# A written-out schedule that counts the port of VectorE and GpSimd, with some work moved between engines

## The chip, the cores and the metric

The kernel runs on one core of a Trainium2 chip. Five engines take part: TensorE (PE, with its weight loads as PEld) multiplies matrices, VectorE (DVE), ScalarE (ACT) and GpSimd (POOL) work element by element, SyncE (SP) issues transfers. Each runs its own instructions in the order in which they were written down and waits for others by semaphores. The metric is device microseconds of one execution; lower is better.

## The reference

Block-sparse attention, whose output is the input of a two-layer network with a Mish-like gate. In short:

```python
scores = (1 / np.sqrt(64)) * q @ k.T                # 4 batches, 8 heads, 768 positions, 64 wide
# block 32; own and neighbouring blocks, first and last row and column of blocks,
# and 3 sampled blocks for each block of queries are kept, the others masked
attn = softmax(np.where(mask, scores, -1e9))
x = (attn @ v).transpose(0, 2, 1, 3).reshape(3072, 512)
h = x @ w_in                                        # 512 x 2048
g = h * np.tanh(np.log1p(np.exp(h)))
out = (g @ w_out).astype(np.float32)                # 2048 x 512
```

q, k and v come as float32, both weights as float64 (two 32-bit words a number).

## The kernel before, in words

Every product is made of float16 matmuls: each factor is scaled by a power of two and split into a high part and a low part (the rest after the high part), and three of the four products are summed. Splitting a number takes a scaling, a cast to float16 and a subtraction, and these steps are shared out among ScalarE, VectorE and GpSimd.

**Attention** is cut into 52 jobs, 13 for each of four batches. A job handles two blocks of 32 queries (or one, "dense", for the first and last block of a batch, over all 768 keys): scores s (L627), maxima mx (L674, dense L669), the negative scaled maximum nb (L685 on ScalarE or L687 on VectorE), exponentials pt (L697), transposes t (L633), high and low parts ph and pl of the transposed weights (L720; L724 on VectorE, or for the first APL jobs a correcting matmul L728 and a copy L733), the product with v into obank (L759), the division xs (L781), a transpose tx, and the parts xh and xl of the network's input (L806, L809). Sampled keys are gathered by GpSimd, for early jobs also by ScalarE, into kg (L564, L561); sampled values by DMAs into vg.

**The weights.** The first (wi) has eight pieces, the second (wo) sixteen. VectorE turns each from float64 into float32 (three steps, L843, L846 and L849). TensorE sums the squares (gram, L327), `root` makes two powers of two from the sum (L358, L361, L235; the same for q, k and v), then each piece is scaled (wt), its high part cast and its low part subtracted. For wi, `split_i` does that by L901 on GpSimd (ScalarE or VectorE where they are freer), L906 or L908, and L910 on GpSimd; pieces with a number below LPE get the subtraction from TensorE instead (wd, L918 and L919) and a copy out of PSUM by ScalarE (L921). For wo it is `parts_o`, with the subtraction L962 on GpSimd. tp_wo is the sum of squares of all of wo: nothing of wo can be scaled, and no second layer begun, before it.

**The network** runs over twelve stages of 256 rows (three a batch): h in 16 halves (L1001, twelve matmuls each), hs, the gate us in five steps on ScalarE, VectorE and GpSimd (L1024 to L1034), g's high and low part (L1042, L1045), and y in 16 halves (L1060). A half of y is of the stage before, and stands between halves of h.

**Order.** All instructions are collected as tasks with a duration, an engine (or several to choose from, "also"), what they read and write, and buffers from rings of fixed size. `Plan.emit` then runs a small model of the engines in the kernel's build and writes out the instructions in the order in which its tasks start; among tasks that can start at the same time the smaller key is first. `pace` spreads the jobs' scores over the network's halves, and delays the first 14 by a table START. Where TensorE would sit idle in the first 200 us of the plan, `fill` writes filler matmuls (L1247) whose result nobody reads. The model's times decide nothing on the chip but the order and the engine.

In the model before, a task marked `port` on VectorE is 1.3 times as long while GpSimd is busy, and a GpSimd task 1.15 times while VectorE is:

```python
if port and free.get("POOL", 0.0) > start:
    t.dur *= 1.3
elif t.eng == "POOL" and free.get("DVE", 0.0) > start:
    t.dur *= 1.15
```

## Time and profile before

| | us |
|---|---|
| timed runs (3): median, lowest, highest | 804.93, 799.87, 806.57 |
| profiled execution: its own time | 797.3 |
| its span, first to last instruction | 795.5 |
| TensorE busy (matmul) | 738.7 (93%) |
| VectorE, ScalarE, GpSimd busy | 522.6, 544.1, 337.2 |

The span is about 2 us shorter than the execution's time. Times in rows are microseconds from the span's start unless marked ns; "x16" counts instructions; L12 is line 12 of the kernel. A row's part after "|" or in brackets is idle time just before these instructions and the instruction that ended most of it. An instruction that holds its engine and is kept from running counts as busy in the profile: it shows as a longer duration, not as idle time.

### The profile page before, as it was taken

To read this page: it belongs to the slowest core of one execution; us is meant where nothing else is said; L and a number is where in the kernel's file an instruction comes from. 1 tells how busy PE (TensorE), PEld (TensorE's weight loads), DVE (VectorE), ACT (ScalarE), POOL (GpSimd) and SP (SyncE) were. 2 spreads that over 40 slices of the span, in tenths; PEclk is the share of its full clock that TensorE was granted. 3 is DMA by queue.
4 is the path that set the end of the run, shared out by engine and by line. 5 is a ranking of instruction groups with operands and counts; after the bars stand their busy time and mean duration, and the time that the engine had idled before them with its cause. 6 is when DMAs were issued, how large, how long until landed. Compare 5 with 4: busy or idle time off the path is not lost.

```text
span 795.5 us, 30849 instructions
## 1 busy us (share of the span) xinstructions
PE 738.7 (93%) x12896; PEld 524.1 (66%) x12896; DVE 522.6 (66%) x904; ACT 544.1 (68%) x859; POOL 337.2 (42%) x392
## 2 busy tenths in 40 slices
PE   6677787699999999999999999998999999999997
PEld 4455576566677776766677676666777667666653
DVE  6689989988976656568576756874776644323230
ACT  3456666788876876887777777877876675555550
POOL 2057775476833534435334543354443421303031
PEclk9899899999999999999999999999999999999999
DMA  8787765405444355235334553263344303000000
GB/s 281 262 256 235 208 205 158 158 2 150 132 119 123 97 162 160 91 83 176 90 81 119 154 160 107 79 180 88 90 117 133 108 25 106 15 14 14 14 14 26
DMA packets 57743, 95.33 MB, mean 120 GB/s; under 512 B 8323, under 2 KB 20612, under 8 KB 57604
## 3 DMA queue, kind: packets, MB, share of 16 engines
q1 hardware_dynamic: 50880, 76.32, 32.7%
q10 hardware_dynamic: 6724, 17.05, 6.6%
q8 instruction: 101, 1.65, 0.9%
q14 instruction: 38, 0.31, 0.1%
HBM read 80.38 MB, written 12.95 MB: 117 GB/s over the span
## 4 chain that ended last, share of the span: by engine, by line
PE 74%; DVE 11%; DMA 7%; issue 3%; ACT 3%; SPq 2%; POOL 1%; ACTq 0%; DVEq 0%; POOLq 0%
PE y L1060 28%; PE h L1001 26%; PE obank L759 6%; PE t L633 6%; PE s L627 4%; DMA raw_q<-in_q_dram 2%; PE obank L1247 1%; PE tx L633 1%; DVE wo L846 1%; DVE wo L849 1%; DVE wt L957 1%; SPq L588 1%; DVE wo L843 1%; DMA vg<-vd 1%; DMA wr<-in_moe_w_in_dram 1%
## 5 line engine op out<-in xcount | busy, mean ns | idle before, releaser
L1001 PE MATMUL h<-xh,wi 128*128 128x256 f16 x1536 | 282.2, 273 | 0.0
L1060 PE MATMUL y<-wo,g 128*128 128x512 f16 x1152 | 277.2, 379 | 0.8 <-POOL wo L962 0.7
L1001 PEld LDWEIGHTS <-wi 128*128 128x128 f16 x2304 | 223.3, 98 | 47.8 <-issue 2.6
L1001 PE MATMUL h<-xl,wi 128*128 128x256 f16 x768 | 209.3, 273 | 0.6 <-issue 0.6
L1045 POOL TENSOR_TENSOR g<-hs,g 128x1024 f16<-128x1024 f32 x48 | 109.9, 2290 | 222.5 <-DVE g L1042 186.7
L1060 PEld LDWEIGHTS <-g 128*128 128x128 f16 x1152 | 110.6, 98 | 101.8 <-issue 3.4
L564 POOL COPY kg<-kt 128x256 f16 x249 | 117.6, 510 | 121.4 <-PE s L627 113.7
L1010 ACT ACTIVATE hs<-h,gsc 128x512 f32<-128x512 f32 x96 | 65.6, 684 | 80.9 <-PE h L1001 73.4
L697 ACT ACTIVATE pt<-s,nb,ns 128x256 f32<-128x256 f32 (+1 forms) x208 | 107.1, 583 | 6.7 <-DVE wi L908 3.2
L720 ACT ACTIVATE ph<-t 128x512 f16<-128x512 f32 x112 | 66.7, 596 | 49.8 <-PE t L633 45.5
L724 DVE SCALAR_TENSOR_TENSOR pl<-t,ph 128x512 f16<-128x512 f32 x97 | 66.2, 684 | 43.7 <-ACT ph L720 43.6
L1034 DVE SCALAR_TENSOR_TENSOR hs<-us,hs 128x1024 f32<-128x1024 f32 x48 | 63.7, 1328 | 28.4 <-ACT us L1033 27.9
L633 PE MATMUL t<-ident,pt 128*128 128x128 f32 x448 | 70.5, 281 | 4.7 <-ACT pl L733 2.4
L1028 DVE TENSOR_SCALAR us<-us 128x1024 f32<-128x1024 f32 x48 | 39.3, 819 | 44.9 <-ACT us L1024 44.9
L633 PEld LDWEIGHTS t<-ident,pt 128*128 128x128 f32 x448 | 51.6, 142 | 18.2 <-ACT pl L733 3.9
L759 PEld LDWEIGHTS <-ph 128*32 128x32 f16 x3584 | 48.2, 95 | 18.9 <-issue 13.5
L674 DVE TENSOR_REDUCE mx<-s 128x4 f32<-128x1024 f32 x44 | 53.3, 1212 | 6.0 <-PE s L627 6.0
L1030 POOL TENSOR_TENSOR us<-us 128x1024 f32<-128x1024 f32 x18 | 36.3, 2018 | 47.3 <-DVE us L1028 41.7
L1024 ACT ACTIVATE us<-hs,hsc 128x1024 f32<-128x1024 f32 x48 | 55.2, 1149 | 1.5 <-DVE hs L1034 0.5
L759 PE MATMUL obank<-vg,ph 128*32 128x65 f16 (+1 forms) x3200 | 50.6, 197 | 2.7 <-issue 2.7
L1032 ACT ACTIVATE us<-us 128x1024 f32<-128x1024 f32 x48 | 50.7, 1055 | 3.0 <-POOL us L1030 2.1
L627 PEld LDWEIGHTS <-q 64*32 64x32 f16 x3024 | 33.7, 92 | 28.6 <-issue 24.9
(201 smaller groups left out, 970.9 us busy)
## 6 DMA issues: line engine op xcount, KB each, us to landing
vg<-vd SPq DMA_DIRECT2D x320, 65.0 KB, 2.4
vg<-vd SPq DMA_DIRECT2D x80, 195.0 KB, 3.0
wr<-in_moe_w_in_dram ACTq DMA_DIRECT2D x8, 1024.0 KB, 7.0
wor<-in_moe_w_out_dram ACTq DMA_DIRECT2D x16, 512.0 KB, 6.5
vd<-v SPq DMA_DIRECT2D x12, 520.0 KB, 3.9
vg<-vd SPq DMA_DIRECT2D x12, 520.0 KB, 4.3
raw_k<-in_k_dram SPq DMA_DIRECT2D x12, 512.0 KB, 5.2
raw_q<-in_q_dram SPq DMA_DIRECT2D x12, 512.0 KB, 4.4
```

Of the source, the lines that this page charges most:

```text
L564: nc.gpsimd.tensor_copy(out=dst, in_=tl["kt", b][:, :, ds(j, BS)])
L627: nc.tensor.matmul(s[g][i * BS:(i + 1) * BS, c0 + cs.start:c0 + cs.stop], q[gs, c * NPR + i, qs], src[gs, a * NPR + i, ks], start=first an ...
L633: nc.tensor.matmul(out, src, ident, start=start, stop=stop, is_transpose=True)
L697: ex = lambda o, x, g, w: nc.scalar.activation(out=o, in_=x, func=AF.Exp, bias=nb[:, g, w:w + 1], scale=tl["ns", b, sus[w]["qb"] // TB][:, ...
L720: nc.scalar.activation(out=new(sb, "ph", ("ph", i, j), [P, 2, 2, P], F16), in_=tl["t", i, j], func=AF.Copy, scale=PSC)
L724: nc.vector.scalar_tensor_tensor(out=new(sb, "pl", ("pl", i, j), [P, 2, 2, P], F16), in0=tl["t", i, j], scalar=PSC, in1=tl["ph", i, j], op ...
L759: nc.tensor.matmul(o[cs, w, g, 0:v1 - v0], p[:, k, g, cs], vt[:, k, 2 * c + g, v0:v1], start=j == 0 and g == 0 and k == 0 and n == 0, stop ...
L1001: nc.tensor.matmul(h[:, f2].rearrange("p (s q) -> p s q", q=BS), wi[:, fp, w, cc, fs], x[:, :, cc], start=f2 == 0 and k == 0, stop=f2 == 1 ...
L1010: nc.scalar.activation(out=tl[kq][:, 2 * (fp % 2):2 * (fp % 2) + 2], in_=tl[kh], func=AF.Copy, scale=gsc[:, fp:fp + 1])
L1034: add("DVE", 1.32, lambda: nc.vector.scalar_tensor_tensor(out=hs(), in0=us(), scalar=-0.5, in1=hs(), op0=ALU.add, op1=ALU.mult), r=[ku], w ...
L1045: add("POOL", 2.3, lambda: nc.gpsimd.tensor_tensor(out=g()[:, 1], in0=hs(), in1=g()[:, 0], op=ALU.subtract), r=[kq, ("gh", b, t, k)], w=[kg])
L1060: nc.tensor.matmul(tl[ky], tl["g", b, t, k][:, g, f, q], wo[:, fc, w], start=fc == 0 and n == 0, stop=fc == NFC - 1 and n == 2)
```

## The change

- The model knows a port: a task of VectorE marked `port` and every task of GpSimd start only when the other engine's held task has ended (or at the end of a small part of it, for a task made of several short ones: `port=0.4`). The factors 1.3 and 1.15 go. Some durations and the model of DMA queues are corrected, and more alternatives of VectorE are marked.
- nb is always made by ScalarE.
- `root` writes the masked exponent back into PSUM and takes both powers from there, so that each of its three steps reads PSUM; before, two read SBUF.
- Scaling wi is done by ScalarE or VectorE, no more by GpSimd; LPE is 10, so that all eight pieces of wi get their low parts by TensorE's subtraction and ScalarE's copy.
- The low parts of wo may be made by VectorE.
- Numbers: WHOLE 14 to 13 (first job whose window of keys is copied by VectorE), APL 7 to 4, START, the keys AT0, ATV and ATP, and for the second batch the jobs at which k, v and q are prepared, PREP (8, 2, 7) to (7, 1, 6): counted from a batch's end, so each one job later.

```diff
-        t = Task({eng: (dur, fn, port), **{e: (d, f, False) for e, d, f in also}}, key, lat, new, kind, len(self.tasks))
+        t = Task({eng: (dur, fn, port or (eng == "POOL" and dur)), **{e: (d, f, o) for e, d, f, o in also}}, key, lat,
+                 new, kind, len(self.tasks))
...
+    def port(held, eng, start, port):
+
+        other = {"DVE": "POOL", "POOL": "DVE"}.get(eng)
+        if port and other in held:
+            at, dur, grain = held[other]
+            if at <= start < at + dur:
+                return at + dur if grain is True else min(at + dur, start + grain)
+        return start
...
-                    start = max(at, f)
+                    start = self.port(held, eng, max(at, f), t.ways[eng][2])
...
+            if port:
+                held[t.eng] = start, t.dur, port
...
-            if port and free.get("POOL", 0.0) > start:
-                t.dur *= 1.3
-            elif t.eng == "POOL" and free.get("DVE", 0.0) > start:
-                t.dur *= 1.15
...
-        nc.vector.tensor_scalar(
-            out=inv.bitcast(I32), in0=tl[key].bitcast(I32), scalar1=1, scalar2=EXPO,
-            op0=ALU.logical_shift_right, op1=ALU.bitwise_and)
-        nc.vector.tensor_single_scalar(
-            inv.bitcast(I32), inv.bitcast(I32), float((64 + sq) << 23), op=ALU.add)
-        pow2_scale(inv, scale)
+        e = tl[key].bitcast(I32)
+        nc.vector.tensor_scalar(out=e, in0=e, scalar1=1, scalar2=EXPO, op0=ALU.logical_shift_right, op1=ALU.bitwise_and)
+        nc.vector.tensor_single_scalar(inv.bitcast(I32), e, float((64 + sq) << 23), op=ALU.add)
+        nc.vector.tensor_scalar(out=scale.bitcast(I32), in0=e, scalar1=-1.0, scalar2=float((267 - 64 - sq) << 23),
+                                op0=ALU.mult, op1=ALU.add)
...
-    WHOLE = 14
+    WHOLE = 13
     SPLIT = 11
-    APL = 7
+    APL = 4
...
-        add("ACT", 0.25 * len(wq), lambda: nb_fn("ACT"), r=[kmx] + [("ns", b, t) for t in qts], w=[("nb", i)],
-            new=[("nb", ("nb", i))], key=-1.5, also=[("DVE", 0.35 * len(wq), lambda: nb_fn("DVE"))])
+        add("ACT", 0.28 * len(wq), nb_fn, r=[kmx] + [("ns", b, t) for t in qts], w=[("nb", i)],
+            new=[("nb", ("nb", i))], key=-1.5)
...
-        add("POOL", 1.4, lambda: t_fn("POOL"), r=[ksc, ("wi", k)], w=[kt], new=[("raw", kt)], key=cls,
-            also=[("ACT", 1.16, lambda: t_fn("ACT")), ("DVE", 0.8, lambda: t_fn("DVE"))])
+        add("ACT", 1.16, lambda: t_fn("ACT"), r=[ksc, ("wi", k)], w=[kt], new=[("raw", kt)], key=cls,
+            also=[("DVE", 0.75, lambda: t_fn("DVE"), True)])
...
-        add("POOL", 1.45, lambda: nc.gpsimd.tensor_tensor(out=wo[:, fc, 1], in0=tl[kt], in1=wo[:, fc, 0],
-                                                          op=ALU.subtract), r=[kt], w=[("wo", fc)], key=cls)
+        sub = lambda eng: eng.tensor_tensor(out=wo[:, fc, 1], in0=tl[kt], in1=wo[:, fc, 0], op=ALU.subtract)
+        add("POOL", 1.2, lambda: sub(nc.gpsimd), r=[kt], w=[("wo", fc)], key=cls,
+            also=[("DVE", 0.7, lambda: sub(nc.vector), True)])
...
-    LPE = 1
-    AT0, ATV, ATW = -15.0, -19.0, 1.0
+    LPE = 10
+    AT0, ATV, ATW = -24.0, -7.0, 1.0
...
-            PREP = (6, 4, 3) if b else (8, 2, 7)
+            PREP = (6, 4, 3) if b else (7, 1, 6)
...
-            LOADO, ATO, ATP = [("dec", 6)], -1.0, -15.0
+            LOADO, ATO, ATP = [("dec", 6)], -1.0, -26.0
...
-    RES, START = 155.0, [0, 66, 57, 72, 72, 57, 99, 72, 15, 12, 9, 24, 6, 18]
+    RES, START = 155.0, [0, 48, 48, 63, 60, 39, 84, 81, 30, 42, 9, 30, 45, 63]
```

More of the change, by code (lines that the diff above doesn't have):

```diff
@@ L145, in emit @@
             if t.kind and t.kind[0] == "dma":
-                dma[t.eng] = max(dma.get(t.eng, 0.0), end) + t.kind[1]
+                other = max([x for e, x in dma.items() if e != t.eng], default=0.0)
+                at = max(dma.get(t.eng, 0.0), end)
+                dma[t.eng] = at + t.kind[1] + min(t.kind[1], 0.5 * max(other - at, 0.0))
                 t.end = max(dma[t.eng], end + t.lat)
@@ L231, in attn_mish_kernel @@
     nc.scalar.preload_act_table_set("natural_log_exp_and_others")
-    def pow2_scale(inv, scale):
-        nc.vector.tensor_scalar(
-            out=scale.bitcast(I32), in0=inv.bitcast(I32),
-            scalar1=-1.0, scalar2=float(267 << 23), op0=ALU.mult, op1=ALU.add)
     offk = const.tile([1, NB * NR], I32, name="offk")
@@ L489, in parts @@
             add("ACT", 1.13, lambda: scaled("ACT"), r=[ks], w=[kr], key=cls,
-                also=[("POOL", 1.15, lambda: scaled("POOL"))])
+                also=[("POOL", 1.15, lambda: scaled("POOL"), 1.15)])
             add("ACT", 1.07, lambda: hi_of("ACT"), r=[kr] + ([("ends",) + key] if what == "v" else []), w=[kh],
@@ L493, in parts @@
                 use=use + ([key] if what != "k" else []), key=cls,
-                also=[("DVE", 0.8, lambda: hi_of("DVE"))])
+                also=[("DVE", 0.75, lambda: hi_of("DVE"), True)])
             add("POOL", 2.15, lo_of, r=[kr, kh], w=[key, ("done",) + key], use=use, key=cls)
@@ L565, in gather_k @@
         add("POOL", 0.53 * NR, lambda: fn("POOL"), r=KT3(b) + ["off"], w=[("kg", n)], use=[("kt", b)], key=-3,
-            also=[("ACT", 0.55 * NR, lambda: fn("ACT"))] if su["early"] else ())
+            port=0.4, also=[("ACT", 0.55 * NR, lambda: fn("ACT"), False)] if su["early"] else ())
         if su["whole"]:
@@ L569, in gather_k @@
                 out=kgs[n][:, :, 0:WK], in_=tl["kt", b][:, :, (qb - 1) * BS:(qb + 2) * BS]),
-                r=KT3(b), w=[("kw", n)], use=[("kt", b)], key=-2)
+                r=KT3(b), w=[("kw", n)], use=[("kt", b)], key=-2, port=True)
     def gather_v(su):
@@ L899, in t_fn @@
                 nc.scalar.activation(out=t, in_=a0_i(k), func=AF.Copy, scale=sc())
[L900 to L901 removed]
             else:
                 nc.vector.tensor_scalar(out=t, in0=a0_i(k), scalar1=sc(), scalar2=None, op0=ALU.mult)
[L904 to L905 removed]
+        add("ACT", 1.16, lambda: t_fn("ACT"), r=[ksc, ("wi", k)], w=[kt], new=[("raw", kt)], key=cls,
+            also=[("DVE", 0.75, lambda: t_fn("DVE"), True)])
         add("ACT", 1.1, lambda: nc.scalar.activation(out=hi, in_=tl[kt], func=AF.Copy), r=[kt],
             w=[("wi", k), ("wih", k)], key=cls,
[L908 removed]
+            also=[("DVE", 0.75, lambda: nc.vector.tensor_copy(out=hi, in_=tl[kt]), True)])
         if k >= LPE:
@@ L931, in load_o @@
         add("ACT", 0.45, lambda: load_w(sb, raw, "raw", w_out.rearrange("(c p) f -> p c f", p=P)[:, fc], a0_o(fc)),
-            r=after, w=[raw, ("wo", fc)], new=[("raw", raw)], key=-5, lat=2.0, kind=("dma", 2.2))
+            r=after, w=[raw, ("wo", fc)], new=[("raw", raw)], key=-5, lat=2.0, kind=("dma", 1.95))
     def piece_o(fc, cls):
@@ L1030, in moe_g @@
         add("POOL", 2.0, lambda: nc.gpsimd.tensor_tensor(out=us(), in0=us(), in1=us(), op=ALU.mult), w=[ku],
-            also=[("ACT", 1.07, lambda: nc.scalar.activation(out=us(), in_=us(), func=AF.Square))])
+            also=[("ACT", 1.07, lambda: nc.scalar.activation(out=us(), in_=us(), func=AF.Square), False)])
         add("ACT", 1.07, lambda: nc.scalar.activation(out=us(), in_=us(), func=AF.Ln, bias=1.0), w=[ku])
@@ L1043, in moe_g @@
         add("DVE", 0.75, lambda: g_fn("DVE"), port=True, r=[kq, "open"], w=[("gh", b, t, k)], new=[("g", kg)],
-            also=[("ACT", 1.07, lambda: g_fn("ACT"))])
+            also=[("ACT", 1.07, lambda: g_fn("ACT"), False)])
         add("POOL", 2.3, lambda: nc.gpsimd.tensor_tensor(out=g()[:, 1], in0=hs(), in1=g()[:, 0], op=ALU.subtract),
@@ L1078, in moe_y @@
             add("DVE", 0.76, lambda: ys_fn("DVE"), r=[ky, ("osc", b)], w=[kys], new=[("ys", kys)], key=-3,
-                also=[("ACT", 0.7, lambda: ys_fn("ACT"))])
+                also=[("ACT", 0.7, lambda: ys_fn("ACT"), False)])
             add("SP", 0.4, out_fn, r=[kys], lat=2.0, kind=("dma", 1.1))
```

29 lines of the change are left out of this document (11 added, 18 removed).

## The prediction

> **What bounds the kernel now.** I read the stretches first. In the windows view the columns are busy time of TensorE (matmul, then weight load), VectorE, ScalarE and GpSimd, with the count of instructions behind each, the granted TensorE clock, the DMA share and GB/s.
>
> ```profile
> core 0: us, PE busy (x) PEld busy (x) DVE busy (x) ACT busy (x) POOL busy (x), PEclk, DMA share, GB/s
> 0.00:50.00 50.00, 32.06 (x602) 25.82 (x603) 34.16 (x84) 22.45 (x39) 9.81 (x26) 0.93 0.82 269
> 50.00:151.00 101.00, 76.31 (x1965) 59.47 (x1962) 94.30 (x145) 65.48 (x120) 65.72 (x58) 0.93 0.68 203
> 151.00:160.25 9.25, 8.30 (x121) 7.40 (x121) 7.89 (x16) 7.39 (x15) 6.38 (x4) 1.00 0.34 117
> 160.25:796.00 635.75, 622.04 (x10216) 431.44 (x10215) 386.27 (x662) 448.74 (x687) 255.26 (x305) 1.00 0.33 95
> ```
>
> There are two regimes. From 160.25 us on TensorE is busy for 622.04 of 635.75 us: only 13.7 us are to be had there, and what VectorE or GpSimd do in it is covered. Before that VectorE is the full engine, 94.30 of 101 us between 50 and 151, while it turns both weight matrices into f32 and serves ten jobs of attention. So the end is the moment at which TensorE becomes full, plus some 636 us of work that stays. These rows of the TensorE timeline date that moment: the scale of the second weight (tp_wo), filler matmuls behind it, and the first matmul of the second layer.
>
> ```profile
> 150.79 0.38 PE L353 MATMUL tp_wo<-am_wo,ones 128*128 128x1 f32 x2
> ...
> 153.21 3.34 PE L1247 MATMUL obank<-neg 128*128 128x240 f16 x31 [0.71 <-DVE xs L781]
> ...
> 160.25 1.46 PE L1060 MATMUL y<-wo,g 128*128 128x512 f16 x6
> ```
>
> Next I read what VectorE's 94.30 us hold, in the groups of 50 to 151 us by form (count | busy us, mean ns).
>
> ```profile
> L849 DVE SCALAR_TENSOR_TENSOR wo<-wor,wo 128x512 int32<-128x512 int32 x16 | 17.1, 1082 | 0.0
> L846 DVE SCALAR_TENSOR_TENSOR wo<-wor,wo 128x512 int32<-128x512 int32 x16 | 16.3, 1028 | 0.0
> L843 DVE TENSOR_SCALAR wo<-wor 128x512 int32<-128x512 int32 x16 | 13.2, 835 | 3.8 <-DMA wor<-in_moe_w_out_dram 3.7
> ...
> L849 DVE SCALAR_TENSOR_TENSOR wi<-wr,wi 128x1024 int32<-128x1024 int32 x4 | 7.0, 1746 | 0.0
> ...
> L361 DVE TENSOR_SCALAR iv_i<-iv_i 128x2 int32<-128x2 int32 x3 | 3.2, 1061 | 0.1
> ...
> L687 DVE TENSOR_SCALAR nb<-mx,ns 128x2 f32<-128x2 f32 x2 | 2.2, 1148 | 0.0
> ```
>
> The same forms, when nothing is in their way, in VectorE's timeline (start us, us):
>
> ```profile
> 49.63 0.18 DVE L361 TENSOR_SCALAR iv_i<-iv_i 128x2 int32<-128x2 int32 x1
> ...
> 61.20 1.23 DVE L849 SCALAR_TENSOR_TENSOR wi<-wr,wi 128x1024 int32<-128x1024 int32 x1
> ...
> 100.23 0.68 DVE L846 SCALAR_TENSOR_TENSOR wo<-wor,wo 128x512 int32<-128x512 int32 x1
> ...
> 105.19 0.22 DVE L687 TENSOR_SCALAR nb<-mx,ns 128x4 f32<-128x4 f32 x1
> ...
> 129.20 0.41 DVE L843 TENSOR_SCALAR wo<-wor 128x512 int32<-128x512 int32 x1
> ```
>
> Group by group, busy less count times the short form: L849 wo 17.1 - 16 x 0.68 = 6.2, L846 wo 16.3 - 10.9 = 5.4, L843 wo 13.2 - 16 x 0.41 = 6.6, L849 wi 7.0 - 4 x 1.23 = 2.1, L361 3.2 - 3 x 0.18 = 2.7, L687 2.2 - 2 x 0.22 = 1.8. That is 24.8 us in which VectorE holds an instruction and does not run it. What it waits for shows where the two timelines are laid side by side:
>
> ```profile
> 70.43 3.08 POOL L910 TENSOR_TENSOR wi<-wt_i,wi 128x1024 f16<-128x1024 f32 x1
> ```
>
> ```profile
> 71.46 2.21 DVE L687 TENSOR_SCALAR nb<-mx,ns 128x2 f32<-128x2 f32 x2
> ```
>
> Two scalings of 128x2 numbers end at 73.67, just behind GpSimd's subtraction, which ends at 73.51. So an instruction of one engine stands still while the other holds what they share. GpSimd's groups between 50 and 151 us:
>
> ```profile
> L564 POOL COPY kg<-kt 128x256 f16 x36 | 20.8, 608 | 10.0 <-PE s L627 7.6 <-POOL kg L564 1.3 <-issue 0.6
> L910 POOL TENSOR_TENSOR wi<-wt_i,wi 128x1024 f16<-128x1024 f32 x7 | 17.6, 2521 | 6.1 <-ACT wi L906 4.1 <-DVE wi L908 2.1
> L901 POOL TENSOR_SCALAR wt_i<-wi,ws 128x1024 f32<-128x1024 f32 x8 | 12.4, 1558 | 2.8 <-DVE wo L849 2.2 <-DVE r L778 0.3 <-DVE ws L235 0.3
> L1030 POOL TENSOR_TENSOR us<-us 128x1024 f32<-128x1024 f32 x3 | 6.0, 1990 | 5.1 <-DVE us L1028 5.1
> L488 POOL TENSOR_TENSOR q<-raw_q,q 128x1024 f16<-128x1024 f32 x2 | 5.1, 2540 | 1.0 <-DVE q L484 1.0
> L1045 POOL TENSOR_TENSOR g<-hs,g 128x1024 f16<-128x1024 f32 x2 | 4.3, 2131 | 7.3 <-DVE wo L849 6.0 <-DVE g L1042 1.2
> ```
>
> **The change, part by part.** *First weight's low parts.* All eight pieces now go the way that one went: GpSimd loses L910 (17.6 us) and L901 (12.4). On GpSimd, in the stretch where pieces 6 and 7 stood, before and then after (wt_i a scaled piece, q a query tile, kg gathered keys; the changed file's line numbers are up to nine higher):
>
> ```order
> L564 COPY kg_111<-kt_237 128x8x32
> L901 TENSOR_SCALAR wt_i_3510<-wi,ws_3303 128x1024
> L901 TENSOR_SCALAR wt_i_3538<-wi,ws_3303 128x1024
> L488 TENSOR_TENSOR q_2_3542<-raw_q_2_2212,q_2_3542 128x1024
> L910 TENSOR_TENSOR wi<-wt_i_3510,wi 128x1024
> ```
>
> ```order
> L571 COPY kg_111<-kt_228 128x8x32
> L480 TENSOR_SCALAR raw_q_2_2252<-raw_q_2_2252,sc_q_2_3543 128x1024
> L495 TENSOR_TENSOR q_2_3643<-raw_q_2_2252,q_2_3643 128x1024
> L540 TENSOR_LOAD offk
> L571 ISA
> ```
>
> The long instructions of the weight are gone; one scaling of a query (ScalarE's before) has come. Up to tp_wo, counted in the two orders, GpSimd also does one L1030 less and 9 copies more. On TensorE the subtractions take places where fillers (neg) stood; the place is behind the transpose of the third job's output (tx), before and after:
>
> ```order
> L728 LDWEIGHTS neg
> L728 MATMUL t_0_2019<-ph_0_2124,neg 128x512
> L633 MATMUL tx_2174<-ident,xs_2015 128x128 x2
> L1247 LDWEIGHTS neg
> L1247 MATMUL obank<-neg 128x240
> ```
>
> ```order
> L640 MATMUL tx_2205<-ident,xs_2082 128x128 x2
> L919 MATMUL wd_0_2209<-wt_i_1858,ident 128x512
> L920 LDWEIGHTS neg
> L920 MATMUL wd_0_2209<-wi,neg 128x512
> L640 MATMUL t_1_2245<-ident,pt_1980 128x128 x4
> ```
>
> So real work replaces fillers, ahead of the next job's transposes (t). Its price, with ScalarE's copies:
>
> ```profile
> 58.38 1.12 PE L918 MATMUL wd<-wt_i,ident 128*128 128x512 f32 x2
> 59.34 0.38 PE L919 MATMUL wd<-wi,neg 128*128 128x512 f16 x1
> ```
>
> ```profile
> L906 ACT ACTIVATE wi<-wt_i 128x1024 f16<-128x1024 f32 x5 | 5.3, 1056 | 0.0
> L685 ACT ACTIVATE nb<-mx,ns 128x4 f32<-128x4 f32 (+1 forms) x9 | 2.5, 289 | 2.1 <-DVE mx L672 2.1
> ...
> L921 ACT ACTIVATE wi<-wd 128x512 f16<-128x512 f32 x2 | 1.3, 630 | 0.0
> ```
>
> A half piece holds TensorE from 58.38 to 59.72, 1.34 us; 14 more make 19 us. Up to 160.25 TensorE is idle for 160.25 - 32.06 - 76.31 - 8.30 = 43.6 us, and the order before holds 186 fillers there at 3.34/31 = 0.11 us, 20 us more. That cover of 64 us hides the 19; without it they would cost 19. ScalarE gets 14 x 0.63 = 8.8 us, 6 scaled pieces at about 1.06 (the nearest row, L906) and 3 more nb at 0.29, and loses 6 pl, 9 gathers and 2 L906: a few us net on an engine busy for 88 of 151.
>
> *Maxima on ScalarE alone, powers of two from PSUM.* VectorE loses nb; behind its mx stands one ScalarE instruction more (0.29) ahead of the exponentials, in a queue with room. On VectorE, behind the third pair of pieces, before and after (tp_w the sum in PSUM, iv_i and ws the two powers, wr and wor raw weights):
>
> ```order
> L687 TENSOR_SCALAR nb_2334<-mx_2208,ns_0_299 128x2
> L687 TENSOR_SCALAR nb_2334<-mx_2208,ns_1_1336 128x2
> L908 CAST wi<-wt_i_2126 128x1024
> L849 SCALAR_TENSOR_TENSOR wi<-wr_1684,wi 128x1024
> L778 TENSOR_SCALAR r_2421<-obank 128x4
> L779 RECIPROCAL r_2421<-r_2421 128x4
> L781 TENSOR_TENSOR xs_2424<-obank,r_2421 128x256
> L358 TENSOR_SCALAR iv_i<-tp_w_2321 128x2
> L361 TENSOR_SCALAR iv_i<-iv_i 128x2
> L235 TENSOR_SCALAR ws_2440<-iv_i 128x2
> ```
>
> ```order
> L781 TENSOR_SCALAR r_2434<-obank 128x4
> L782 RECIPROCAL r_2434<-r_2434 128x4
> L784 TENSOR_TENSOR xs_2437<-obank,r_2434 128x256
> L846 TENSOR_SCALAR wo<-wor_2254,wo 128x512
> L849 SCALAR_TENSOR_TENSOR wo<-wor_2254,wo 128x512
> L367 TENSOR_SCALAR tp_w_2376<-tp_w_2376 128x2
> L368 TENSOR_SCALAR iv_i<-tp_w_2376 128x2
> L369 TENSOR_SCALAR ws_2471<-tp_w_2376 128x2
> L852 SCALAR_TENSOR_TENSOR wo<-wor_2254,wo 128x512
> ```
>
> nb is gone, the three steps of the powers all read PSUM, and the second weight's decode has moved up around them. What reading PSUM costs on 128x2 numbers:
>
> ```profile
> L358 DVE TENSOR_SCALAR iv_i<-tp_w 128x2 int32<-128x2 int32 x3 | 0.4, 147 | 0.0
> ```
>
> 147 ns from PSUM against 0.18 us from SBUF in the L361 row above: no dearer, so I book 0 for the move and count the blocked 2.7 us under the port. [...]
>
> *What VectorE takes on.* Up to tp_wo the order after has, of the forms below, 6 pl more, 7 xl (4 of them half size), one xs, 2 scalings and 2 casts of 1024 columns, and one us (0.68), one hs, one cast of q (0.68) and three nb (0.22) less.
>
> ```profile
> L1034 DVE SCALAR_TENSOR_TENSOR hs<-us,hs 128x1024 f32<-128x1024 f32 x3 | 3.6, 1213 | 0.0
> ...
> L724 DVE SCALAR_TENSOR_TENSOR pl<-t,ph 128x512 f16<-128x512 f32 x6 | 4.1, 677 | 0.0
> L781 DVE TENSOR_TENSOR xs<-obank,r 128x256 f32<-128x256 f32 x8 | 3.4, 424 | 0.3
> ...
> L908 DVE CAST wi<-wt_i 128x1024 f16<-128x1024 f32 x3 | 2.0, 681 | 0.0
> ...
> L809 DVE TENSOR_TENSOR xl<-tx,xh 128x256 f16<-128x256 f32 x1 | 0.4, 408 | 0.0
> ```
>
> 6 x 0.68 + (4 x 0.25 + 3 x 0.41) + 0.7 (0.42 and its two small steps) + 4 x 0.68 = 9.7; less 0.68 + 1.21 + 0.68 + 0.66 = 3.2. Net 6.5 us more.
>
> *What the port gives back.* GpSimd's long instructions (all groups above but the copies) sum to 45.4 us; after, 45.4 - 17.6 - 12.4 - 2.0 + 1.1 = 14.5, a ratio of 0.32. With the copies, 65.72 falls to about 65.72 - 30.0 - 2.0 + 1.1 + 9 x 0.6 = 40, a ratio of 0.61. Waiting left on VectorE: 24.8 x 0.32 = 8 to 24.8 x 0.61 = 15. I take 11, nearer to the long ones, since a copy lasts 0.6 us and cannot hold anybody for 2. Given back: 24.8 - 11 = 14 (10 to 17). That the plan now moves work out of a hold's way is not booked separately; a bad guess of it costs no more than the upper end.
>
> *From tp_wo to the first y.* Before, 9.5 us pass, with two halves of h (twelve matmuls each) and 37 fillers. After, no filler and four halves stand there, since two fewer are done by tp_wo (14 of 18). What a half takes, in the chain that ended last:
>
> ```profile
> 764.32 1.31 PE h L1001 x12
> ```
>
> Without a wait four halves take 5.2 us; with the waits of before, which the halves then fill, it stays 9.5. I take the middle, 7.3: 2.2 less.
>
> *The rest.* Five of sixteen low parts of the second weight go to VectorE, two y-evacuations and squares change engines, preparation of the second batch starts one job later: all behind 160 us, where TensorE waits 13.7 us in all; I book 0, with 3 us either way. The cover there is VectorE's 250 idle us; if the later preparation failed it, TensorE would wait on v of the second batch, which the order after has moved one job back as well.
>
> **Sum.** 6.5 - 14 - 2.2 = -9.7, so TensorE is full at about 150.5 instead of 160.25. VectorE's idle 15.8 of the first 50 us, in which it waits for loads and TensorE, I leave as it is, with 5 us either way for the new order. The profiled execution took 797.3 us (795.5 from first to last instruction): 797.3 - 9.7 = 787.6. The three timed runs lie 2.6 to 9.3 above it, their median 7.6, so I predict 795.
>
> **Rivals.** *The gain turns into another wait (0.32).* L843 already waits 3.7 us for the second weight's transfers, which land in a ring of six tiles that scaled pieces use too; the DMA share is 0.82, then 0.68. A VectorE that is 8 us quicker finds them not there; what stays is 0 to 5 us: 792 to 797 profiled, 800 to 805 as a median. For it speaks that row, against it that 3.7 of 151 us is little.
>
> *Slower: pieces 6 and 7 come late (0.13).* GpSimd finished the last piece early:
>
> ```profile
> 117.48 2.13 POOL L910 TENSOR_TENSOR wi<-wt_i,wi 128x1024 f16<-128x1024 f32 x1
> ```
>
> at 119.6, 31 us ahead of tp_wo. After, they are scaled, cast, subtracted and copied near the end of the front, in queues that run in order: 2 x 1.06 + 1.06 + 4 x 1.34 + 4 x 0.63 = 11 us, plus as much of ScalarE's exponentials standing between, 22 in all; the first layer's products need them, and behind those stands everything on TensorE. If they are 24 us late against need, 797.3 - 9.7 + 24 = 811.6, median 819. It decides from 18 us late (9.7 + 8) on. For it: their place in the order. Against it: VectorE's decode is still running then and is itself the later one.
>
> *The change misses its aim (0.05):* waits stay at 24.8 us because VectorE's decode with two SBUF inputs meets copies instead: 6.5 - 2.2 = 4 us more, 801.6 profiled, 809.
>
> **Chances.** The forecast's case has 0.50, its own range 783 to 801 as a median (10 to 17 given back, 5.2 to 9.5, and the 5 and 3 us left open). About 1% (8 us) is what a measurement of this kernel can tell from no change: faster below 797, slower above 813. Faster: 0.42 of the forecast's 0.50 and 0.05 of the first rival, 0.47. Slower: the second rival's 0.12 and a little of the third, 0.13. Same: 0.40. The range of 782 to 809 leaves out 0.06 below (all waits gone) and 0.13 above.
>
> **What would show it.** Right: L1060 starts near 150.5; L843, L846 and L849 of wo near 0.45, 0.75 and 0.75 us mean; GpSimd busy about 40 us in the stretch before tp_wo; TensorE's idle time after the first y still near 14 us. Wrong: the same means with L843 waiting on wor for 10 us (first rival); h waiting behind wd or L921's copies (second); L849 of wo still above 1 us (third). A TensorE that idles over 20 us after the first y would break the assumption that the rest stays.

## The result, and the profile after

The changed kernel takes 795.75 us (median of seven executions, 792.79 to 796.49), the kernel before, on the same chip, 803.21 (796.62 to 806.57): a ratio of 0.9899, with a 95% interval of 0.9865 to 0.9934. A second series gave 794.33 us and 0.9896 [0.9862, 0.993]. Two single executions of the series below were slow ones (868.18 us with the first matmul of each wd out, 794.91 us with squares and loads later); the medians in the table include them, the ratios do not. So the change is about 1% faster, at the border of what I had called "faster", and the forecast of 795 us is met. The sum behind it is not: I had forecast 787.6 us for the profiled execution, and it took 795.1, only 2.2 less than the one before; a second pair of profiles, below, differs by 6.5.

The first view of after is the page's head and its busy times.

```profile
span 793.4 us, 30780 instructions
PE 745.1 (94%) x12869; PEld 526.1 (66%) x12869; DVE 491.1 (62%) x895; ACT 551.1 (69%) x881; POOL 305.3 (38%) x386
```

VectorE and GpSimd have lost 31.5 and 31.9 us of busy time (522.6 and 337.2 before), TensorE has 6.4 us more. Next the windows of after, cut at tp_wo and at the first matmul of the second layer (columns as in the prediction), and the two rows of TensorE's timeline that give the cuts.

```profile
0.00:50.00 50.00, 32.68 (x605) 26.80 (x606) 37.17 (x88) 22.27 (x34) 10.41 (x27) 0.93 0.89 287
50.00:153.50 103.50, 84.49 (x1998) 61.70 (x1998) 77.43 (x153) 67.10 (x124) 36.03 (x51) 0.93 0.66 198
153.50:159.06 5.56, 5.56 (x54) 5.02 (x53) 4.16 (x10) 5.40 (x11) 3.97 (x2) 1.00 0.09 33
159.06:794.00 634.94, 622.40 (x10218) 432.60 (x10215) 372.38 (x646) 456.29 (x714) 254.89 (x307) 1.00 0.33 95
```

```profile
153.46 0.28 PE L360 MATMUL tp_wo<-am_wo,ones 128*128 128x1 f32 x2
...
159.06 1.46 PE L1062 MATMUL y<-wo,g 128*128 128x512 f16 x6
```

The rest behind the first y is what it was: 622.40 us of TensorE work where it was 622.04. What differs in this pair lies in front. There VectorE's busy time fell from 34.16 + 94.30 = 128.5 to 37.17 + 77.43 = 114.6 us, but tp_wo comes 2.7 us later than before: VectorE's idle time up to tp_wo rose from 22.5 to 38.9 us. Only the way from tp_wo to the first y became shorter, 9.5 to 5.6 us. VectorE's groups of 50 to 153.5 us show both halves of this (count | busy us, mean ns | idle time before, and what ended it):

```profile
L852 DVE SCALAR_TENSOR_TENSOR wo<-wor,wo 128x512 int32<-128x512 int32 x16 | 12.1, 760 | 0.0
L849 DVE SCALAR_TENSOR_TENSOR wo<-wor,wo 128x512 int32<-128x512 int32 x16 | 11.8, 740 | 0.1
L846 DVE TENSOR_SCALAR wo<-wor 128x512 int32<-128x512 int32 x16 | 8.8, 551 | 3.4 <-DMA wor<-in_moe_w_out_dram 3.4
L681 DVE TENSOR_REDUCE mx<-s 128x4 f32<-128x1024 f32 x7 | 8.5, 1220 | 4.4 <-PE s L634 4.4
L727 DVE SCALAR_TENSOR_TENSOR pl<-t,ph 128x512 f16<-128x512 f32 x12 | 8.2, 685 | 13.2 <-ACT ph L723 13.1
L852 DVE SCALAR_TENSOR_TENSOR wi<-wr,wi 128x1024 int32<-128x1024 int32 x4 | 5.4, 1362 | 0.0
...
L368 DVE TENSOR_SCALAR iv_i<-tp_w 128x2 int32<-128x2 int32 x3 | 0.5, 159 | 0.1
L367 DVE TENSOR_SCALAR tp_w<-tp_w 128x2 int32<-128x2 int32 x3 | 0.5, 159 | 0.4 <-PE tp_w L358 0.4
L369 DVE TENSOR_SCALAR ws<-tp_w 128x2 int32<-128x2 int32 x3 | 0.4, 149 | 0.0
```

The waits at the port are nearly gone. By the prediction's own short forms, the decode of wo is over by 12.1 - 10.9 = 1.2, 11.8 - 10.9 = 0.9 and 8.8 - 6.6 = 2.2 us, that of wi (L852) by 0.5, and the scalings of 128x2 numbers by nothing: 4.8 us, where it had been 24.8. But VectorE now stands 13.1 us in front of pl, waiting for a ph of ScalarE; before, that wait did not show. GpSimd's groups of the same stretch:

```profile
L571 POOL COPY kg<-kt 128x256 f16 x44 | 23.5, 543 | 35.5 <-PE s L634 27.5 <-POOL kg L571 5.2 <-issue 1.8
L1032 POOL TENSOR_TENSOR us<-us 128x1024 f32<-128x1024 f32 x2 | 4.5, 2271 | 2.6 <-DVE us L1030 2.6
L1047 POOL TENSOR_TENSOR g<-hs,g 128x1024 f16<-128x1024 f32 x2 | 4.3, 2132 | 9.5 <-ACT g L1042 6.6 <-DVE g L1044 2.9
L495 POOL TENSOR_TENSOR q<-raw_q,q 128x1024 f16<-128x1024 f32 x2 | 4.3, 2131 | 6.3 <-ACT q L489 6.3
```

The 30 us of the first weight are gone, and most of what is left are copies.

Why is ScalarE late? Here are the issue of a load by SyncE (SPq) and the instruction of ScalarE that needs it, first in the timeline of before, then of after. raw_q is the first tile of queries of the second batch, L318 and L325 sum its squares.

```profile
95.14 0.41 SPq L385 DMA_DIRECT2D raw_q<-in_q_dram  x1
...
102.70 1.06 ACT L318 ACTIVATE I-3366_3367<-raw_q 128x1024 f16<-128x1024 f32 x1 [1.34 <-DMA raw_q<-in_q_dram]
```

```profile
102.30 0.41 SPq L392 DMA_DIRECT2D raw_q<-in_q_dram  x1
...
109.73 1.06 ACT L325 ACTIVATE I-3422_3423<-raw_q 128x1024 f16<-128x1024 f32 x1 [6.76 <-DMA raw_q<-in_q_dram]
...
111.40 0.69 DVE L727 SCALAR_TENSOR_TENSOR pl<-t,ph 128x512 f16<-128x512 f32 x1 [4.72 <-ACT ph L723]
```

By the numbers in `load` the plan reckons under 3 us from issue to landing (0.5 to issue, then 1.95 of transfer or 2.0 of latency, whichever ends later), and puts the squares right behind that. On the chip this load takes 7.4 us, and in after it leaves SyncE 7.2 us later than before, behind gathers of vg. ScalarE had ended its other work at 102.97. It is held at the head of its queue by a transfer, while the ph behind it could have run from 105.5 us on, when its transposes were done; and VectorE, which reaches pl in its own order, stands too, for 4.7 of its 13.1 us (another 5.5 lie at 85 us, behind a second stand of ScalarE that comes further down).

The ph is not all that stands behind the squares: so do three of ScalarE's issues of w_out loads, which left at 109.8 and 110.8. The chain of work that ended last goes by these loads (start us, us, what):

```profile
102.30 7.41 DMA raw_q<-in_q_dram
109.82 3.79 DMA wor<-in_moe_w_out_dram
113.63 0.43 DVE wo L846
...
117.58 4.31 PE h L1003 x24
...
128.20 2.73 PE h L1003 x24
```

The last two rows are two halves of h each, so the same work: the first pair took 1.6 us longer, at a granted clock of 0.61; the second ran at 1.00. That ScalarE's stand is what the gain went into was the theory to test.

### The profile page after: what moved, and what is told of

Its sections match the earlier page's. It is cut to its first block, busy times and chain, and to the rows that moved or that the text cites. A ratio compares the mean times of both kernels' runs of the same rounds, so it can differ in the third digit from the quotient of the medians.

```text
span 793.4 us, 30780 instructions
## 1 busy us (share of the span) xinstructions
PE 745.1 (94%) x12869; PEld 526.1 (66%) x12869; DVE 491.1 (62%) x895; ACT 551.1 (69%) x881; POOL 305.3 (38%) x386
## 3 DMA queue, kind: packets, MB, share of 16 engines
q1 hardware_dynamic: 50880, 76.32, 32.6%
## 4 chain that ended last, share of the span: by engine, by line
PE 79%; DVE 7%; DMA 6%; ACT 3%; issue 3%; POOL 2%; SPq 0%; POOLq 0%; ACTq 0%; DVEq 0%
PE y L1062 29%; PE h L1003 28%; PE t L640 6%; PE obank L762 6%; PE s L634 5%; DMA raw_q<-in_q_dram 3%; DMA vg<-vd 2%; PE tx L640 1%; PE obank L1249 1%; DVE hs L1036 1%; POOL wo L963 1%; DMA raw_k<-in_k_dram 1%; DVE wt L958 1%; PE gram_wi L334 1%; DVE wo L852 1%
## 5 line engine op out<-in xcount | busy, mean ns | idle before, releaser
L1047 POOL TENSOR_TENSOR g<-hs,g 128x1024 f16<-128x1024 f32 x48 | 106.2, 2214 | 202.6 <-DVE g L1044 152.6
L571 POOL COPY kg<-kt 128x256 f16 x258 | 114.8, 480 | 170.7 <-PE s L634 156.0
L727 DVE SCALAR_TENSOR_TENSOR pl<-t,ph 128x512 f16<-128x512 f32 x103 | 70.7, 687 | 62.5 <-ACT ph L723 62.2
L1036 DVE SCALAR_TENSOR_TENSOR hs<-us,hs 128x1024 f32<-128x1024 f32 x48 | 66.7, 1391 | 31.9 <-ACT us L1035 31.8
L1032 POOL TENSOR_TENSOR us<-us 128x1024 f32<-128x1024 f32 x19 | 39.2, 2062 | 40.1 <-DVE us L1030 40.1
L1034 ACT ACTIVATE us<-us 128x1024 f32<-128x1024 f32 x48 | 50.7, 1056 | 1.9 <-POOL us L1032 1.3
L1035 ACT ACTIVATE us<-us 128x1024 f32<-128x1024 f32 x48 | 50.7, 1056 | 0.9
```

The lines of the kernel that those rows point to most:

```text
L571: nc.gpsimd.tensor_copy(out=dst, in_=tl["kt", b][:, :, ds(j, BS)])
L727: nc.vector.scalar_tensor_tensor(out=new(sb, "pl", ("pl", i, j), [P, 2, 2, P], F16), in0=tl["t", i, j], scalar=PSC, in1=tl["ph", i, j], op ...
L1036: add("DVE", 1.32, lambda: nc.vector.scalar_tensor_tensor(out=hs(), in0=us(), scalar=-0.5, in1=hs(), op0=ALU.add, op1=ALU.mult), r=[ku], w ...
L1047: add("POOL", 2.3, lambda: nc.gpsimd.tensor_tensor(out=g()[:, 1], in0=hs(), in1=g()[:, 0], op=ALU.subtract), r=[kq, ("gh", b, t, k)], w=[kg])
```

## The experiments

The medians and ratios to the kernel before are of the same series in each row; tp_wo, the first y, the halves of h that TensorE has done by then and its idle time before and behind it are from one profiled execution each.

| kernel | median us | ratio [95% interval] | tp_wo, first y | halves of h | idle before, behind |
|---|---|---|---|---|---|
| before, its first profile | 803.21 | | 150.8, 160.3 | 18 | 43.6, 13.2 |
| before again | 800.54 | 0.9987 [0.9959, 1.0016] | 154.5, 164.0 | 18 | 42.8, 13.1 |
| after | 795.75 | 0.9899 [0.9865, 0.9934] | 153.5, 159.1 | 18 | 36.3, 11.9 |
| after again | 794.33 | 0.9896 [0.9862, 0.993] | 150.8, 156.4 | 18 | 32.1, 11.9 |
| low parts moved, all else as before | 800.78 | 0.9974 [0.9945, 1.0003] | 134.9, 150.3 | 15 | 35.8, 13.0 |
| after, low parts back on GpSimd | 812.29 | 1.0139 [1.01, 1.0177] | 156.2, 167.8 | 16 | 45.5, 16.0 |
| after, port not in the plan | 804.63 | 1.004 [1.0012, 1.0069] | 140.8, 147.2 | 13 | 32.6, 22.8 |
| after, numbers of before | 798.42 | 0.9973 [0.9941, 1.0005] | 142.3, 147.4 | 9 | 33.7, 14.3 |
| after, first matmul of each wd out | 792.74 | 0.9868 [0.979, 0.9946] | 152.8, 158.4 | 18 | 44.2, 10.6 |
| after, squares of another tile | 788.27 | 0.9818 [0.9756, 0.9879] | 148.8, 154.4 | 18 | 30.3, 13.9 |
| after, squares later | 787.05 | 0.9833 [0.9798, 0.9869] | 143.6, 149.2 | 18 | 29.5, 12.0 |
| the same, a second series | 787.41 | 0.9844 [0.9805, 0.9883] | 146.3, 151.9 | 18 | 32.7, 11.2 |
| after, two loads later | 793.59 | 0.9892 [0.9854, 0.993] | 151.6, 157.2 | 18 | 32.4, 12.1 |
| after, squares and loads later | 790.11 | 0.9868 [0.9823, 0.9912] | 143.0, 148.6 | 18 | 28.0, 10.8 |

**The two kernels once more.**

> The kernel before, unchanged. Its timed runs spread from 796.6 to 806.6 us and its profiled execution (797.3) is one of the quick ones. Theory A (the gain lies in the front): ratio 1.000 within 0.004; a second profile shows the first y (L1060) somewhere between 158 and 172 us, and from there to the end 634 to 639 us again, as 635.75 us in the first profile, so that what differs between executions lies ahead of the first y. Theory B (the gain lies behind the first y): the first y again near 160 us, and the stretch behind it longer than 640 us when the execution is slow.

> The changed kernel, unchanged, for a second profile: both theories 0.990 of the kernel before (0.986 to 0.994). Theory A: first y between 156 and 162 us, the rest 634 to 636 us. Theory B: the rest under 634 us.

Profiles of the same kernel differ in front (the first y at 160.3 and 164.0 for before, 159.1 and 156.4 for after) and hardly behind it (635.2 and 634.9; 634.3 and 636.0). So the profile that I started from was a quick execution of before, and the difference of 2.2 us between the two first profiles is less than the 7.5 us between the medians. In the second pair tp_wo comes 3.7 us earlier with the change, where it came 2.7 us later in the first, and the first y 7.6 us earlier instead of 1.2; VectorE's idle time up to tp_wo rises by 10.0 us (26.7 to 36.7) instead of 16.4. The granted clock differs too: from 50 us to tp_wo it was 0.93 in the first profile of before, 0.85 in the second. It is the medians that count below; a single profile tells where, not how much.

**The moved low parts alone**, in the kernel before:

```diff
-        add("POOL", 1.4, lambda: t_fn("POOL"), r=[ksc, ("wi", k)], w=[kt], new=[("raw", kt)], key=cls,
-            also=[("ACT", 1.16, lambda: t_fn("ACT")), ("DVE", 0.8, lambda: t_fn("DVE"))])
+        add("ACT", 1.16, lambda: t_fn("ACT"), r=[ksc, ("wi", k)], w=[kt], new=[("raw", kt)], key=cls,
+            also=[("DVE", 0.8, lambda: t_fn("DVE"))])
...
-    LPE = 1
+    LPE = 10
```

> The kernel before with one part of the change: all eight pieces of the first weight get their low parts from TensorE and ScalarE, and GpSimd no longer scales them; planner, constants, nb and root as before. Theory A: VectorE's decode of the second weight falls to about 0.75, 0.75 and 0.55 us mean (L849, L846, L843; before 1.08, 1.03 and 0.84), and the time to 0.990 to 0.996. Theory C (the planner's model and its numbers make the gain, the first weight is a detail): 0.998 to 1.010, with the plan unfit for the new work on ScalarE.

VectorE's groups of wo in this kernel, 50 to 155 us:

```profile
L846 DVE SCALAR_TENSOR_TENSOR wo<-wor,wo 128x512 int32<-128x512 int32 x16 | 11.4, 719 | 0.0
L849 DVE SCALAR_TENSOR_TENSOR wo<-wor,wo 128x512 int32<-128x512 int32 x16 | 11.4, 720 | 0.0
L843 DVE TENSOR_SCALAR wo<-wor 128x512 int32<-128x512 int32 x16 | 10.1, 631 | 7.2 <-DMA wor<-in_moe_w_out_dram 7.2
```

The waits at the port fall by this move alone, without a plan that knows the port, and tp_wo comes 16 us earlier than before, at 134.9. That is worth nothing measurable: from tp_wo to the first y 15.4 us now pass, and behind the first y there are 649 us instead of 635, since only 15 halves of h, not 18, are done by then. The first y dates the end only between orders that have the same work ahead of it.

**The rest of the change alone**, the low parts back on GpSimd:

```diff
+            elif eng == "POOL":
+                nc.gpsimd.tensor_scalar(out=t, in0=a0_i(k), scalar1=sc(), scalar2=1.0, op0=ALU.mult, op1=ALU.mult)
...
-        add("ACT", 1.16, lambda: t_fn("ACT"), r=[ksc, ("wi", k)], w=[kt], new=[("raw", kt)], key=cls,
-            also=[("DVE", 0.75, lambda: t_fn("DVE"), True)])
+        add("POOL", 1.4, lambda: t_fn("POOL"), r=[ksc, ("wi", k)], w=[kt], new=[("raw", kt)], key=cls,
+            also=[("ACT", 1.16, lambda: t_fn("ACT"), False), ("DVE", 0.75, lambda: t_fn("DVE"), True)])
...
-    LPE = 10
+    LPE = 1
```

> The changed kernel with that part undone: GpSimd scales and subtracts the first weight again (one piece by TensorE), the rest of the change kept, port in the plan included. Theory A: decode means back above 0.9 us, time 0.996 to 1.004 of the kernel before. Theory C: the plan moves the work out of the port's way, decode means 0.75 or less, time 0.988 to 0.994.

Slower by 1.4%, which no theory had: the plan and its numbers do not carry the gain, and without the moved low parts they harm. Yet most of the waits at the port are gone here as well: the decode means are 0.55, 0.71 and 0.87 us, and against the short forms the decode of wo and L852 of wi are about 7 us over, where the same four groups of before were 20.3. So in two kernels, by the move alone and by the plan alone, VectorE got most of these waits back, and neither is measurably faster than before.

**The plan without the port**, and **the numbers of before**:

```diff
-                    start = self.port(held, eng, max(at, f), t.ways[eng][2])
+                    start = max(at, f)
...
+            if t.eng == "DVE" and port and free.get("POOL", 0.0) > start:
+                t.dur *= 1.3
+            elif t.eng == "POOL" and free.get("DVE", 0.0) > start:
+                t.dur *= 1.15
```

> The kernel after, but the planner knows the port as in the kernel before: the start of an instruction is not put off, and its duration is stretched by 1.3 (VectorE) or 1.15 (GpSimd) where the other engine is busy. All operations, the first weight's low parts by TensorE and all constants as in after; only the order moves. Theory P (the plan's knowledge of the port is what makes the moved low parts pay): ratio to before 0.996 to 1.004, VectorE's decode steps in 50 to 150 us back above 0.85 us in the mean, or waits elsewhere that cost as much. Theory Q (knowing the port does nothing once GpSimd has little to do; the numbers and the moved work do it): ratio 0.987 to 0.993, decode steps at 0.55, 0.75 and 0.75 us as in after.

```diff
-    WHOLE = 13
+    WHOLE = 14
...
-    APL = 4
+    APL = 7
...
-    AT0, ATV, ATW = -24.0, -7.0, 1.0
+    AT0, ATV, ATW = -15.0, -19.0, 1.0
...
-            PREP = (6, 4, 3) if b else (7, 1, 6)
+            PREP = (6, 4, 3) if b else (8, 2, 7)
...
-            LOADO, ATO, ATP = [("dec", 6)], -1.0, -26.0
+            LOADO, ATO, ATP = [("dec", 6)], -1.0, -15.0
...
-    RES, START = 155.0, [0, 48, 48, 63, 60, 39, 84, 81, 30, 42, 9, 30, 45, 63]
+    RES, START = 155.0, [0, 66, 57, 72, 72, 57, 99, 72, 15, 12, 9, 24, 6, 18]
```

> The kernel after, but with the numbers of the kernel before for the start of the jobs, the classes of the first weight's pieces and of the second weight's, the job at which the next batch is prepared, and which jobs gather on ScalarE or on VectorE (START, AT0, ATV, ATP, PREP, APL, WHOLE); the first weight's low parts by TensorE and the port in the plan as in after. Theory Q (the numbers had to follow the moved work: what is gained from the port is lost again in the order): ratio to before 0.995 to 1.005, first y at 163 to 168. Theory P (the plan's knowledge of the port makes the order good by itself): ratio 0.987 to 0.993, first y at 156 to 160.

Both lose all or most of the gain. The ratios came out as theory P had it for the first and theory Q for the second, but of the mechanisms only P's alternative, waits elsewhere, can be seen; theory Q's first y of 163 to 168 us came at 147.4. Moved work, plan and numbers pay only together. Without the port in the plan the decode of wo stays at 0.48, 0.74 and 0.83 us, so the port is not what is lost; the order is another one, with the first y at 147.2 but 13 halves of h before it, and TensorE idle for 22.8 us behind it, where after has 11.9. Each of these edits writes out a new order, so they cannot say more of a single cause. The runs below therefore keep the order of after, instruction for instruction, but for what they name.

**Does TensorE's extra work cost the gain?**

```diff
-                nc.tensor.matmul(d, ident, tl[kt][:, cs], start=True, stop=False)
-                nc.tensor.matmul(d, neg[:, 0], hi[:, cs], start=False, stop=True)
+                nc.tensor.matmul(d, neg[:, 0], hi[:, cs], start=True, stop=True)
```

> The kernel after, in the same order on every engine, but of each pair of matmuls that forms low parts of the first weight in PSUM the first one (identity times t in f32: two passes of 0.59 us each, 32 passes in all, 18.9 us of TensorE) is left out; the low parts are then minus the high parts, so the output is another. ScalarE's copies out of PSUM and everything else stay. Theory D (before the first y TensorE has no idle time to spare for that work; 12.8 us more of it is what the freed port time was paid with): the first y starts 9 to 14 us earlier than in after (at 145 to 150), ratio to before 0.971 to 0.979. The prediction's own step (that work lies under 64 us of idle time and fillers, and costs nothing) and theory E: TensorE idles instead, the first y moves by less than 3 us, ratio 0.986 to 0.992.

The kernel leaves out a product, so its output is another one. The extra work does not cost the gain: the first y of the profile is at 158.4, the median 2 to 3 us lower, and the interval holds after's ratio. (TensorE's busy time fell by 9.6 us, not by 18.9. Up to the first y many of the matmuls that are left took longer, the 131 fillers 20.9 us instead of 18.1, with a granted clock of 0.88 instead of 0.94, so this does not say what the removed ones had taken.) In its place TensorE idles, and its clock is granted less in this profile. Windows of 50 to 100 us, after and then this kernel:

```profile
50.00:100.00 50.00, 40.54 (x1133) 27.95 (x1133) 37.55 (x77) 32.57 (x69) 19.24 (x32) 0.93 0.70 205
```

```profile
50.00:100.00 50.00, 30.23 (x1038) 22.57 (x1038) 34.73 (x74) 28.86 (x61) 17.47 (x29) 0.80 0.69 201
```

**Is it the wait for raw_q?** First the squares read a tile that is there:

```diff
-            squares(tl["raw", what, b, j], tl[key][:, k:k + 1])
+            src = tl["raw", what, b, j]
+            if (what, b, j) == ("q", 1, 0):
+                src = tl["kt", 0].rearrange("p r s -> p (r s)")[:, 0:4 * TT]
+            squares(src, tl[key][:, k:k + 1])
```

> The kernel after, in the same order on every engine; only the squares of the second batch's first q tile (L325), at which ScalarE stood 6.8 us idle in the profile of after (the load of raw_q was not there), read the first batch's k tile, which has long been there, in place of raw_q. So the scale of that q tile, and with it the output, is another; the work is the same in kind and number. Theory E (the gain went into the wait of ScalarE for raw_q, behind which the ph of the attention and with them VectorE's pl stand): ScalarE's wait at L325 is gone, VectorE's wait at L727 for ph falls from 13 us to about 8, the first y starts 4 to 6 us earlier (at 153 to 155) and the ratio to before is 0.982 to 0.985. Theory D (the gain went into TensorE's own work on the first weight's low parts): something else takes the wait's place, the first y stays within 2 us of 159, ratio 0.987 to 0.992, as after.

The ratio is 0.9818, at the low end of theory E's range, with the first y at 154.4 and VectorE's wait for ph at 7.2 us, as theory E had them. With four executions the interval reaches into theory D's range as well, and the medians alone (788.27 to 800.81) give 0.984. Then the squares stand later in ScalarE's order, a kernel that computes all that after computes. The plan is made as before; when it comes to write out this one instruction, it holds it back:

```diff
...
-            fn()
+            if t.late:
+                held_back.append([t.late, t.eng, fn()])
+            else:
+                fn()
+                for x in held_back:
+                    x[0] -= t.eng == x[1] and t.dur > 0
+                for x in [x for x in held_back if not x[0]]:
+                    x[2]()
+                    held_back.remove(x)
...
+        later = 6 if (what, b, j) == ("q", 1, 0) else 0
...
```

> The kernel after; nothing is left out. In ScalarE's order the squares of the second batch's first q tile (L325) come six instructions later, behind a ph, an hs and an xh, whose inputs are there while raw_q is still on its way; every other engine's order is as in after. Theory F (what VectorE got back at the port went into ScalarE, which stands at the head of its own queue for transfers: 6.8 us here and 6.6 us before an issue of a w_out load at 76 to 83): ScalarE's wait here falls to under 2 us and the time to that of the kernel that squares another tile, ratio to before 0.981 to 0.986. Theory G (the transfers themselves bound the stretch up to tp_wo, so another engine waits for them instead): ratio 0.988 to 0.992.

> The kernel after with the squares of the second batch's first q tile six instructions later on ScalarE, a second time. If it is faster than after for good: ratio to before 0.981 to 0.986 again, first y at 148 to 152. If the first series was a lucky one: 0.987 to 0.992, as after, first y at 155 to 159.

Rows of the first series' profile: ScalarE's instructions around the squares, the first y, and VectorE's waits up to 150 us (us in total, times, longest).

```profile
105.36 0.69 ACT L1024 ACTIVATE hs<-h,gsc 128x512 f32<-128x512 f32 x1 [1.54 <-PE h L1015]
107.12 0.38 ACT L821 ACTIVATE xh<-tx 128x256 f16<-128x256 f32 x1 [1.07 <-PE tx L652]
107.40 1.05 ACT L335 ACTIVATE I-3601_3602<-raw_q 128x1024 f16<-128x1024 f32 x1
```

```profile
149.20 1.46 PE L1074 MATMUL y<-wo,g 128*128 128x512 f16 x6
```

```profile
DVE wo L858 <- DMA wor<-in_moe_w_out_dram: 5.1, 4, 1.9
DVE pl L739 <- ACT ph L735: 4.3, 3, 3.2
```

The squares no longer wait, the wait before pl is 4.3 us where it was 13.1 (5.9 and 10.1 in the second profiles of the two kernels), and the kernel takes 787 us in both series. That is 5 us less than after by the ratios to before (0.984 against 0.990) and 7 to 9 by the medians, which are of different series: the wait at one instruction, 6.8 and 5.3 us in the two profiles of after, had cost about its length, down to the end. This kernel is faster by 1.6% than before and by about 0.6% than after; the intervals of the two touch, but both series say the same, and a kernel of the same series with another instruction moved, below, takes 6.5 us more.

What of the stand costs, the runs show in part. The squares now stand behind a ph, an hs and an xh, as expected, but also behind the three issues of w_out loads, which the expectation did not name: the first leaves at 101.68 instead of 109.82, and VectorE's decode step behind it starts at 107.45 instead of 113.63. In the second profiles it is 103.79 for 107.43, and 109.75 for 111.11. (At the xs just before, the first was already 2.4 us ahead of after's and the second 0.6 behind; that is the spread between executions.) Between 110 and 120 us the granted clock is 1.00 in both profiles of this kernel, where it was 0.70 and 0.66 in those of after, and the two halves of h behind that step take 2.6 us where they took 4.3 and 4.8. So about 2 us of the 5, an estimate from these two halves, come by way of the clock. The share of the ph and that of the loads are not told apart by any run.

**ScalarE's other stand.** In after ScalarE issues the load of w_out number 5 late, and the instruction behind it waits with it; the page puts the wait down to a gather of vg that landed just before. From ScalarE's timeline, and TensorE's longest wait of 50 to 160 us:

```profile
76.13 0.39 ACT L809 ACTIVATE xh<-tx 128x256 f16<-128x256 f32 x1
82.77 0.82 ACTq L838 DMA_DIRECT2D wor<-in_moe_w_out_dram  x2
83.63 1.09 ACT L922 ACTIVATE wi<-wd 128x512 f16<-128x512 f32 x2 [7.11 <-DMA vg<-vd]
```

```profile
PE gram_wi L334 <- ACT wi L922: 5.5, 1, 5.5
```

The issues of loads 5 and 6 were put eight instructions later in the same way:

```diff
+        later = 8 if fc in (5, 6) else 0
```

> The kernel after; nothing is left out. ScalarE's issues of w_out loads 5 and 6 (L838), the first of which it issued only at 82.8 in the profile of after, when a gather of vg had landed (ScalarE had ended the work before it at 76.5), come eight instructions later in ScalarE's order, behind low parts, a ph, an xl, an nb and two pt; the other engines' orders are as in after. Theory F: ScalarE does that work from 76.5 on, the 7.1 us wait before L922 and TensorE's 5.5 us before the gram_wi at 84.3 fall below 2 us each, the first y comes 3 to 6 us earlier than in after, ratio to before 0.982 to 0.986. Theory G: TensorE then waits for vg there itself, or VectorE for wor; ratio 0.988 to 0.992.

> Both moves in ScalarE's order together: the squares of raw_q six instructions later, the issues of w_out loads 5 and 6 eight later; nothing is left out. Theory F: the two stands are one after the other in time, so what they give adds up: first y at 148 to 153, near the forecast's 150.5, ratio to before 0.972 to 0.980, and VectorE's wait for ph (13.1 us in after) below 5 us. Theory G: one transfer or another is late all the same; ratio 0.984 to 0.992.

Here theory F fails. TensorE's wait of 5.5 us is gone and VectorE's wait for ph is half of what it was, but the time is that of after; the largest waits of TensorE and VectorE up to then are now these:

```profile
PE t L741 <- issue: 4.5, 1, 4.5
PE obank L772 <- issue: 3.6, 2, 2.4
```

```profile
DVE pl L737 <- ACT ph L733: 6.5, 3, 3.8
DVE mx L691 <- PE s L644: 5.6, 4, 3.3
```

Both moves together bring VectorE's wait for ph down to 1.4 us and the first y of the profile to 148.6, but the median is 790.1, no better than the squares alone (the intervals overlap; single executions lie between 782 and 795, and the profiled one is the quickest). In the chains of these two kernels a load of w_out stands at this place, which left at 71.9 and 69.3 us and took 9.0 and 8.5 us: another transfer is late all the same, as theory G had it. What would have to come sooner to gain here was not tried and stays open.

## Why the prediction was right, and where it was wrong

- **Two regimes, and a rest that stays.** Held between before and after: 13.2 and 11.9 us idle behind the first y, with the same 18 halves of h ahead of it. As a rule it is false: in three other orders the first y came at 147 to 150 us, with 9 to 15 halves ahead of it, and the end no sooner than before.
- **VectorE's own work, +6.5, and the port, -14.** The gain was larger than forecast: the six groups kept 4.8 us of their 24.8, so 20 came back (10 to 17 forecast), and VectorE's busy time up to tp_wo fell by 13.9 us (7.5 forecast). I had reckoned the waits in proportion to GpSimd's busy time; GpSimd's 36.0 us (40 forecast) are two thirds copies, and with these alone left beside a few long instructions little waiting remains. The decode means of 0.55, 0.74 and 0.76 us are near the 0.45, 0.75 and 0.75 named.
- **"VectorE's idle 15.8 of the first 50 us ... I leave as it is": the step that failed**, together with the silent one that its 6.7 idle us behind them stay too. I took VectorE for the only limit of the front. Its idle time up to tp_wo grew by 16.4 us in the first pair of profiles and by 10.0 in the second, against 13.9 and 13.7 us less of busy time. So tp_wo came 2.7 us later and 3.7 earlier, not 7.5 earlier. The largest new part is the wait for ph, 13.1 and 10.1 us; of these 4.7 and 3.9 stand behind ScalarE's wait for raw_q, which holds up loads of w_out as well. That this stand costs about 5 us is shown: with it out of the way, and every other engine's order the same, the first y came at 149.2 and 151.9, and the profiled execution took 785.2 and 787.1 us. These are near the 150.5 and 787.6 of the forecast, but not by its sum: VectorE still idles 29.3 and 31.3 us up to tp_wo there, where it idled 22.5 and 26.7 before the change. What the rest of the added idle time costs was not tested.
- **The first rival, "the gain turns into another wait",** is what happened, with its number for the profiled execution (792 to 797; 795.1 and 794.2) but not with its median (800 to 805), and not at its place: L846 waits 3.4 us for wor, L843 waited 3.7 before. I had looked for the new wait at the engine that became faster and at loads that the change did not move. It came at ScalarE, at a load that the change moved: in the part on "the rest" I booked the later preparation at 0, as lying "all behind 160 us", but its first load and squares stand at 102 us.
- **The cover of TensorE's 19 us.** Held as far as it can be told: leaving out most of that work gained 2 to 3 us, which the intervals do not tell from nothing.
- **PSUM for the powers of two.** Held: the three steps took 149 to 159 ns from PSUM in after, where the step on 128x2 numbers that nothing held up took 0.18 us from SBUF in before.
- **tp_wo to the first y, -2.2.** 5.6 us instead of 7.3, near the lower end: -3.9. It is the one part of the front that is shorter by the same amount in both pairs of profiles.
- **The median.** The two errors of the sum, -13.9 for -7.5 and +16.4 for 0, left -1.2 at the first y in the first pair of profiles, where -9.7 stood; in the second pair it was -7.6. By the medians of the two series the change gained 7.5 and 7.4 us. My forecast went from 804.93 to 795, a gain of 9.9, too much by 2.5. And 804.93 was the median of three executions; the later series of before have medians of 800.2 to 803.2, so the start was too high by about as much. The two errors cancel, and that 795 came out is partly luck.
